# Token-mixing MLP beside attention: a scheduler that reckons weight loads 1.8 times as long, and its searched rules

## The chip, the cores and the metric

The kernel runs on one core of one Trainium2 chip. The metric is the device time of a launch in microseconds. A core has the engines PE (TensorE, matrix products), DVE (VectorE), ACT (ScalarE), POOL (GpSimd) and SP (SyncE, which here issues all transfers). Each has its own instruction queue, worked off in order; they meet only at semaphores.

## The reference

A layer norm without parameters feeds two branches, which are multiplied and added to the input. All tensors are bfloat16; S = 2048 tokens, D = 640, H = 32 heads of 20, F = 1536.

```python
def _A_ref(x, wqkv, wo):                       # attention
    qkv = (x @ wqkv).reshape(B, S, 3, H, Dh).transpose(2, 0, 3, 1, 4)
    q, k, v = qkv[0], qkv[1], qkv[2]
    scores = einsum("bhqd,bhkd->bhqk", q, k) * (Dh ** -0.5)
    p = softmax(scores, axis=-1)
    o = einsum("bhqk,bhkd->bhqd", p, v)
    return o.transpose(0, 2, 1, 3).reshape(B, S, D) @ wo

def _B_ref(x, w1, b1, w2, b2):                 # MLP over the tokens
    h = layernorm(x)
    u = gelu_tanh(einsum("bsd,sf->bdf", h, w1) + b1)
    y = einsum("bdf,fs->bds", u, w2) + b2
    return y.transpose(0, 2, 1)

xn = layernorm(A_x)
out = A_x + _A_ref(xn, A_wqkv, A_wo) * silu(_B_ref(xn, B_w1, B_b1, B_w2, B_b2))
```

The exponentials are the bulk: 32 heads x 2048 x 2048 scores.

## The kernel before

The kernel does not list its instructions in a fixed order. A Python program (the scheduler) runs when the kernel is built: it keeps an estimate of when each engine is free, chooses at each step the next piece of work for the engine that is free first, and so writes one fixed instruction order for each engine. What it decides by its estimates is frozen in these orders; on the chip only the semaphores act.

Scores are computed in units of one head x 128 keys x 512 queries, one bank of the accumulator memory each. There are 2048 such units. Most go to ACT, which takes the exponential of two or three banks in one instruction. 496 of them go to DVE instead, in quads of four heads: DVE converts a bank to a 16-bit number that, read as bfloat16, approximates the exponential (`emit_op1`), and derives from the four banks three shifted copies in one instruction each (`emit_top`); the four approximations are added with weights in the product with v.

```python
    def emit_exp():
        us, banks, grp = pexp.pop(0)
        n = len(us)                                        # 2 or 3 banks
        ...
        tk = pr.act(lambda e: e.activation(outp, inp, AF.Exp, scale=math.log(2.0) / 128.0), ...
                    cost=n * 512 * 0.8335 + 50.0)
    def emit_op1():
        tk = pr.dve(lambda e: e.tensor_scalar(w, src, WOFF, 0.0, ALU.add, ALU.max), ... cost=601.0)
    def emit_top():
        tk = pr.dve(lambda e: e.tensor_scalar(dst, src, dk, None, ALU.add), ... cost=dv(2048, .26))
```

The MLP's products fill PE in between. Its weights come in slices of 256 columns, w1 in six slices and w2 in eight, into two buffers used in turn: the load of slice k waits until the products of slice k - 2 have been read (`wr` holds the buffer's slot).

```python
        def dma_w1(k):
            src = B_w1[:, k * 256:(k + 1) * 256].rearrange("(b p) f -> p b f", p=P)
            dst = w1_ap(k)
            wr = [S_(f"wm{k % 2}")]
            return ("dma", lambda e: e.dma_start(dst, src), [], wr, f"dma_w1_{k}", S * 512,
                    [S_(f"x{b}") for b in range(NB)] if k < 2 else [])
        def dma_w2(k):
            ...
            return ("dma", lambda e: e.dma_start(dst, src), [], wr, f"dma_w2_{k}", F * 512,
                    [S_("wm0"), S_("wm1")] if k < 2 else [])
        ...
            if j % 2 == 1 and j // 2 + 2 < NB // 2:
                k = j // 2 + 2
                add_job(f"w2_{k}", [dma_w2(k), ("tag", f"w2_{k}")], (f"m2_{j}_0", f"m2_{j}_1"), 40.0)
```

The number in the sixth place (S * 512, F * 512) is the load's size in bytes as the scheduler reckons it; the true size is the same (2048 x 256 x 2 bytes for w1, 1536 x 256 x 2 for w2). It becomes a cost, and the cost a landing time. Times are in ns; `pipe` is the one pipe that all transfers share in the reckoning:

```python
        def dma(fn, reads, writes, name, nbytes, over=()):
            if nbytes is None:                             # the transposing DMAs
                pr.dma(fn, ..., cost=1320.0, over=over, tail=3200.0)
            else:
                pr.dma(fn, ..., cost=nbytes / 355.0, over=over)
    # in Prog._add, for a transfer:
            start = max(start, 700.0)
            if tail is not None:
                self.T[eng] = start + cost
                self.pipe = max(self.pipe, start) + cost
                t.fin = self.pipe - cost + tail
            else:
                self.T[eng] = start + 450.0
                self.pipe = max(self.pipe, start + 600.0) + cost
                t.fin = self.pipe + (1200.0 if self.pipe < 2500.0 else 2800.0 if cost > 800.0 else 1400.0)
```

All transfers are issued by SP in the order in which the scheduler made them. Among them are sixteen transposing DMAs, made in one piece when the attention output of the first six head groups is complete:

```python
        def reload_steps():
            steps = []
            for c in range(4):
                for tb in range(NTB):
                    ...
                    steps.append(("dma", lambda e, d=d, src=src: e.dma_start_transpose(d, src), ...))
```

The scheduler's rules of choice have fourteen parameters. A table gives their values for each window of 16 units of scores; each digit chooses one of the values of the option in that place:

```python
    OPTS = (
        ("SLACK", (120.0, 40.0, 200.0, 320.0)),
        ("MINJ", (640.0, 320.0, 1000.0)),
        ("ROOM", (3, 6, 0)),
        ...
        ("GROT", (1, 0)),
    )
    PLAN = (
        "00000000000010", "00000000000000", "00000000000010", ...      # 129 rows
    )
    def tune(self, w):
        if w < len(self.PLAN):
            for (name, vals), i in zip(self.OPTS, self.PLAN[w]):
                setattr(self, name, vals[int(i)])
    # in the main loop of schedule():
            if nclaim[0] >= win * self.WIN:
                self.tune(win)
                win += 1
```

The table was found by a search over the scheduler's own estimate. SLACK, for instance, is how far other PE work may overrun the moment at which ACT will need its next scores.

Of the kernel before, what the change touches and what calls it, by code (L numbers as in the profile page):

```python
# [260 lines left out]
class _Kern:  # L261
# [53 lines left out]
        ("GROT", (1, 0)),  # L315
    )
    PLAN = (
        "00000000000010", "00000000000000", "00000000000010", "00000000000000", "00000410000000", "10010410000100",
        "00004010011000", "20204010111000", "00000000000000", "02000020010010", "00000000000000", "00000010001000",
        "00000000000000", "01000120000000", "01003120000000", "00000000000000", "00000010000100", "00000310100000",  # L320
        "02020320011000", "02020320011000", "02120010011000", "00000220000100", "30000220000100", "02000010000000",
        "00000000000000", "00000000100000", "02000100100100", "01000120001010", "00000000000000", "00003300000000",
        "00000000000000", "01000000000010", "00004000000000", "10011000000000", "01022300000000", "00000000000000",
        "30020100000000", "02000010110000", "00000100000000", "00010100000110", "00001000000000", "20100000000100",
        "11000000000000", "00000000000000", "00001000010000", "10020000000000", "10020000010000", "10020010010000",
        "00000000000000", "22103000000000", "22103010000000", "01220100000100", "00000000000000", "00100000001000",
        "02000000100000", "01000300001000", "01000300001000", "00000000000000", "00100000001000", "00100400100000",
        "01000000001000", "00004000000000", "10002000010000", "01001400001010", "01021420000110", "00000300000000",
        "00000020000010", "00000000000000", "00000010001000", "10000100000000", "10000100000000", "10004100001000",
        "00004120000000", "00001010000000", "10011410000110", "11001200000110", "11001200100110", "00020000000000",  # L330
        "00000000000000", "00000000100100", "00200400100000", "02100010110010", "02101010100010", "01000000000000",
        "01000000000000", "00000000000000", "00000400000000", "00000000000000", "00000020001000", "00020320000000",
        "00000000000000", "01000010000000", "01000010000100", "20000000000100", "02000000000000", "12000000000000",
        "00001000101000", "00000000000000", "00200000010100", "00020020100000", "01003000000000", "22000000000000",
        "21210000000000", "00000000000000", "00200020110000", "00000000000000", "00200000000100", "00000000001000",
        "00020310000100", "00220020000010", "10224000000010", "31223410000010", "30200000000100", "00021000000010",
        "00100000001010", "01100000010010", "01204001000000", "01204100001000", "00204100000010", "02024120000000",
        "02024320000000", "02000200000000", "12000200010000", "00000000000000", "00001000100000", "00001000100000",
        "00000000001000", "10000000000000", "00000000000000",
    )  # L340
    PARTS = (2,)
    DX = (1, 2, 3)
# [74 lines left out]
    def schedule(self):  # L417
        pr, t, nc = self.prog, self.t, self.nc
        S, NB, NTB, F, FC, D, H, DH, NG, GH = (self.S, self.NB, self.NTB, self.F, self.FC, self.D,
                                               self.H, self.DH, self.NG, self.GH)  # L420
# [18 lines left out]
        def S_(name):  # L439
            s = sl.get(name)  # L440
            if s is None:
                s = sl[name] = _Slot(name)
            return s
# [321 lines left out]
        def w1_ap(k):  # L765
            return bass.AP(regA, (k % 2) * NB * 256, [[NB * 640, P], [256, NB], [1, 256]])

        def w2_ap(k):
            return bass.AP(regA, (k % 2) * FC * 256, [[NB * 640, P], [256, FC], [1, 256]])

        def dma_w1(k):
            src = B_w1[:, k * 256:(k + 1) * 256].rearrange("(b p) f -> p b f", p=P)
            dst = w1_ap(k)
            wr = [S_(f"wm{k % 2}")]
            return ("dma", lambda e: e.dma_start(dst, src), [], wr, f"dma_w1_{k}", S * 512,
                    [S_(f"x{b}") for b in range(NB)] if k < 2 else [])

        def dma_w2(k):
            src = B_w2[:, k * 256:(k + 1) * 256].rearrange("(fc p) s -> p fc s", p=P)
            dst = w2_ap(k)  # L780
            wr = [S_(f"wn{k % 2}")]
            return ("dma", lambda e: e.dma_start(dst, src), [], wr, f"dma_w2_{k}", F * 512,
                    [S_("wm0"), S_("wm1")] if k < 2 else [])

        def ztmp(i):
# [652 lines left out]
        for i, (b0, nb) in enumerate(LN):  # L1438
            rq = () if i < 4 else (f"xn{LN[i - 1][0] + LN[i - 1][1] - 1}",)
            steps = ln_steps(b0, nb)  # L1440
            k = next(n for n, x in enumerate(steps) if x == ("tag", f"lnp{b0}")) + 1
# [16 lines left out]
        for w in (1, 0):  # L1458
            src = A_wqkv[:, 640 * w + 256:640 * w + 640].rearrange("(kc p) f -> p kc f", p=P)
# [52 lines left out]
        for G in range(1, NG):  # L1512
            cs = sorted({(80 * G - 80) // 128, (80 * G - 1) // 128})
            for w in (1, 0):
# [4 lines left out]
            add_job(f"vs{G}", vs_steps(G, list(range(NR))), vtag + ((f"pvG{G - 2}",) if G >= 2 else ()), 28.0,  # L1519
                    at=(4 * G - 1.0 if G < NG - 1 else 24.0))  # L1520
        add_job("w1a", [dma_w1(0), dma_w1(1), ("tag", "w1_0"), ("tag", "w1_1")], ("h_all",) + xtall, 40.0)
        ml = []
        for j in range(FC):
            rq = ("h_all", "bias", f"w1_{j // 2}")
            ml.append((f"m1_{j}_0", mlp_steps(1, j, 0), rq, 16 * 216.0))
            if j % 2:
                ml.append((f"m1_{j}_1", mlp_steps(1, j, 1), rq + (f"m1_{j - 1}_0",), 32 * 60.0))
            if j % 2:
                add_job(f"a1_{j}", act_steps(1, j), tuple(f"m1_{i}_{q}" for i in (j - 1, j) for q in (0, 1)), self.ACTP)
            if j % 2 == 1 and j // 2 + 2 < FC // 2:  # L1530
                k = j // 2 + 2
                add_job(f"w1_{k}", [dma_w1(k), ("tag", f"w1_{k}")], (f"m1_{j}_0", f"m1_{j}_1"), 40.0)
        m1all = tuple(f"a1_{j}" for j in range(FC))
        m1pe = tuple(f"m1_{j}_{q}" for j in range(FC) for q in (0, 1))
        add_job("w2a", [dma_w2(0), dma_w2(1), ("tag", "w2_0"), ("tag", "w2_1")], m1pe, 40.0)
        for j in range(NB):
            rq = m1all + (f"w2_{j // 2}",)
            ml.append((f"m2_{j}_0", mlp_steps(2, j, 0), rq, 12 * 216.0))
            if j % 2:
                ml.append((f"m2_{j}_1", mlp_steps(2, j, 1), rq + (f"m2_{j - 1}_0",), 24 * 60.0))  # L1540
            if j % 2:
                add_job(f"a2_{j}", act_steps(2, j), tuple(f"m2_{i}_{q}" for i in (j - 1, j) for q in (0, 1)), self.ACTP)
# [3 lines that stand above are left out]
# [11 lines left out]
        for gb in range(4):  # L1557
            src = A_x[0, gb * 512:(gb + 1) * 512, :].rearrange("(b p) d -> p b d", p=P)
            dst = regA[:, gb * 4:(gb + 1) * 4, :]
# [377 lines left out]
        while True:  # L1937
# [40 lines left out]
            r, e = bt  # L1978
# [46 lines left out]
```

The softmax here doesn't subtract the row's maximum and nothing guards it: scores larger than these inputs give would overflow.

## Time and profile before

| | before |
|---|---|
| time, median of 3 runs | 757.67 us (757.1 to 758.49) |
| span of the profiled run | 756.4 us |
| exps on ACT, two banks / three banks | 434 / 228 |
| conversions on DVE, first / derived | 496 / 372 |
| transfers | 42.54 MB, mean 56 GB/s |

The span is that of one profiled execution. A group of instructions is shown as line, engine, operation, what it writes and reads, shape and count; then the busy time, the mean duration of one in ns, and the idle time of the engine just before them with what ended it. Durations of neighbours can overlap. In a timeline a line holds instructions of one kind merged, with their start, length and count. SPq is the queue of SP.

### The profile page before, as it was taken

To read this page: it belongs to the slowest core of one execution; us is meant where nothing else is said; L and a number is where in the kernel's file an instruction comes from. 1 tells how busy PE (TensorE), PEld (TensorE's weight loads), DVE (VectorE), ACT (ScalarE), POOL (GpSimd) and SP (SyncE) were. 2 spreads that over 40 slices of the span, in tenths; PEclk is the share of its full clock that TensorE was granted. 3 is DMA by queue.
4 is the path that set the end of the run, shared out by engine and by line. 5 is a ranking of instruction groups with operands and counts; after the bars stand their busy time and mean duration, and the time that the engine had idled before them with its cause. 6 is when DMAs were issued, how large, how long until landed. Compare 5 with 4: busy or idle time off the path is not lost.

```text
span 756.4 us, 22917 instructions
## 1 busy us (share of the span) xinstructions
PE 726.6 (96%) x10194; PEld 245.9 (33%) x10194; DVE 718.4 (95%) x1319; ACT 731.3 (97%) x686; POOL 15.7 (2%) x22
## 2 busy tenths in 40 slices
PE   8899999999999999999999989999999899999997
PEld 6332233222332323323232233333333333322232
DVE  7799999999999999999999999999999898999996
ACT  4999999999999999999999999999999999999994
POOL 4200000000000000000000000000000000000001
PEclk9999999999999999999999999999999999999999
DMA  8694111101120302203010131331134510410002
GB/s 240 89 160 88 41 20 37 21 13 30 37 63 12 76 13 44 62 26 76 13 39 13 37 91 31 69 80 29 45 81 76 104 50 2 152 47 29 31 13 70
DMA packets 117143, 42.54 MB, mean 56 GB/s; under 512 B 75300, under 2 KB 115876, under 8 KB 116996
## 3 DMA queue, kind: packets, MB, share of 16 engines
q1 hardware_dynamic: 117044, 41.07, 24.2%
q8 instruction: 80, 1.31, 0.8%
q14 instruction: 19, 0.16, 0.1%
HBM read 26.37 MB, written 10.22 MB: 48 GB/s over the span
## 4 chain that ended last, share of the span: by engine, by line
ACT 67%; PE 23%; SPq 4%; DVE 3%; DMA 3%; POOL 1%; issue 0%; DVEq 0%; ACTq 0%
ACT pt_sb L1241 65%; PE ps_all L1212 7%; PE ps_all L1292 7%; PE ps_all L645 7%; SPq L906 3%; DMA xnT_sb<-regC 1%; PE ps_all L930 1%; DMA regA<-in_B_w_dram 1%; ACT zt_sb L836 1%; DMA wqk_sb<-in_A_wqkv_dram 1%; DVE dt_sb L1252 1%; PE ps_all L630 1%; POOL st_sb L567 0%; SPq L1425 0%; DVE regC L1615 0%
## 5 line engine op out<-in xcount | busy, mean ns | idle before, releaser
L1241 ACT ACTIVATE pt_sb<-ps_all 128x1024 bf16<-128x1024 f32 (+1 forms) x662 | 711.5, 1212 | 3.9 <-PE ps_all L1212 2.9
L1252 DVE TENSOR_SCALAR dt_sb<-ps_all 128x512 uint16<-128x512 f32 x496 | 330.8, 681 | 17.1 <-PE ps_all L1212 15.6
L1212 PE MATMUL ps_all<-qk_sb 32*128 32x512 bf16 x2048 | 286.6, 384 | 18.7 <-ACT pt_sb L1241 14.5
L1276 DVE TENSOR_SCALAR dt_sb<-dt_sb 128x2048 uint16<-128x2048 uint16 x372 | 245.9, 684 | 1.6
L1212 PEld LDWEIGHTS ps_all<-qk_sb 32*128 32x128 bf16 x2048 | 73.9, 91 | 276.4 <-ACT pt_sb L1241 193.0
L1292 PE MATMUL ps_all<-pt_sb,v_sb 128*21 128x512 bf16 x1552 | 123.6, 382 | 1.0 <-DVE v_sb L1045 1.0
L1292 PE MATMUL ps_all<-dt_sb,vs_sb 128*21 128x512 bf16 x1488 | 123.6, 381 | 0.3 <-DVE dt_sb L1276 0.2
L645 PE MATMUL ps_all<-regB,regA 128*32 128x128 bf16 (+1 forms) x1536 | 66.8, 301 | 1.5 <-DMA regA<-in_B_w_dram 1.2
L645 PE MATMUL ps_all<-regC,regA 128*32 128x512 bf16 (+1 forms) x1536 | 65.9, 301 | 0.0
L1292 PE MATMUL ps_all<-dt_sb,v_sb 128*21 128x512 bf16 x496 | 48.9, 385 | 0.6 <-DVE tr_sb L1408 0.3
L645 PE MATMUL ps_all<-xnT_sb,wqk_sb 128*32 128x512 bf16 x640 | 48.9, 382 | 0.3 <-DVE v_sb L1045 0.2
L1292 PEld LDWEIGHTS ps_all<-pt_sb,v_sb 128*21 128x21 bf16 x1552 | 29.1, 90 | 50.6 <-issue 38.5
L1292 PEld LDWEIGHTS ps_all<-dt_sb,vs_sb 128*21 128x21 bf16 x1488 | 31.6, 91 | 38.2 <-issue 18.8
L645 PEld LDWEIGHTS ps_all<-regB,regA 128*32 128x32 bf16 x1536 | 28.1, 96 | 28.5 <-issue 12.2
L645 PEld LDWEIGHTS ps_all<-regC,regA 128*32 128x32 bf16 x1536 | 28.5, 96 | 25.7 <-issue 11.7
L930 PE MATMUL ps_all<-wv_sb,xnT_sb 128*128 128x128 bf16 (+3 forms) x160 | 30.1, 302 | 0.1
L645 PE MATMUL ps_all<-wv_sb,xnT_sb 128*32 128x480 bf16 x320 | 23.6, 369 | 0.2 <-DVE v_sb L1045 0.2
L1408 DVE STREAM_TRANSPOSE tr_sb<-ps_all 128x512 f32<-128x512 f32 x31 | 21.9, 707 | 0.0
L645 PEld LDWEIGHTS ps_all<-xnT_sb,wqk_sb 128*32 128x32 bf16 x640 | 14.3, 95 | 20.0 <-issue 8.7
L1292 PEld LDWEIGHTS ps_all<-dt_sb,v_sb 128*21 128x21 bf16 x496 | 12.4, 90 | 23.7 <-issue 18.3
L815 DVE TENSOR_SCALAR zt_sb<-ps_all,b2h_sb 128x512 bf16<-128x512 f32 (+1 forms) x32 | 17.2, 543 | 1.4 <-PE ps_all L645 1.2
L1045 DVE CAST v_sb<-ps_all 128x480 bf16<-128x480 f32 (+1 forms) x24 | 14.3, 594 | 2.3 <-PE ps_all L738 2.1
(81 smaller groups left out, 291.0 us busy)
## 6 DMA issues: line engine op xcount, KB each, us to landing
regA<-in_B_w_dram SPq DMA_DIRECT2D x6, 1024.0 KB
regA<-in_B_w_dram SPq DMA_DIRECT2D x8, 768.0 KB
qk_sb<-qk_scratch_dram SPq DMA_DIRECT2D x56, 80.0 KB
qk_scratch_dram<-qs_sb SPq DMA_DIRECT2D x32, 128.0 KB
regA<-in_A_x_dram SPq DMA_DIRECT2D x6, 640.0 KB
ok_scratch_dram<-on_sb SPq DMA_DIRECT2D x96, 20.0 KB
out_dram<-regC SPq DMA_DIRECT2D x3, 640.0 KB
wqk_sb<-in_A_wqkv_dram SPq DMA_DIRECT2D x2, 480.0 KB
```

The source lines that it names most:

```text
L630: steps.append(("pe", lambda e, dc=dc, lhsT=lhsT: e.matmul(ps(bk, n), lhsT, xnT_sb[:, dc, tb * 512 + c0:tb * 512 + c0 + n], start=(dc == 0 ...
L645: fns.append(lambda e, c=c, e_=e_: e.matmul(oc(c, e_), lhsT[:, c:e_], rhs, start=start, stop=stop, tile_position=(0, c)))
L815: steps.append(("dve", lambda e, z=z, i=i, jj=jj: e.tensor_scalar(z[:, c0:c0 + n], ps(bk, n, i * n), 0.5, bias[:, jj:jj + 1], ALU.mult, AL ...
L906: steps.append(("dma", lambda e, d=d, src=src: e.dma_start_transpose(d, src), [S_(f"okd{pass_of[(G, tb)]}_{g}") for G in range(L6) for g i ...
L930: steps.append(("pe", lambda e, c=c, k=k: e.matmul(ap, oT_sb[0:k, c, b * 128:(b + 1) * 128], wo_ap[0:k, c, c0:c0 + n], start=(opens and c ...
L1045: return lambda e: e.tensor_copy(dst, src)
L1212: pr.pe(lambda e, outp=outp, lhsT=lhsT, rhs=rhs, g=g: e.matmul(outp, lhsT, rhs, start=True, stop=True, tile_position=(32 * g, 0)), reads=[ ...
L1241: tk = pr.act(lambda e: e.activation(outp, inp, AF.Exp, scale=math.log(2.0) / 128.0), reads=[bank_slot[b] for b in banks[:n]], writes=[S_( ...
L1252: tk = pr.dve(lambda e: e.tensor_scalar(w, src, WOFF, 0.0, ALU.add, ALU.max), reads=[bank_slot[bk]], writes=[S_(f"dt{d['tl'][0]}_{g}")], n ...
L1276: tk = pr.dve(lambda e: e.tensor_scalar(dst, src, dk, None, ALU.add), reads=[S_(f"dt{b0}_{g}") for g in range(4)], writes=[S_(f"dt{b}_{g}" ...
L1292: pr.pe(lambda e: e.matmul(outp, lhsT, rhs, start=(k == 0), stop=last, tile_position=(0, 32 * g)), reads=reads, writes=[bank_slot[AB]], na ...
L1408: steps.append(("dve", lambda e: e.transpose(tr_sb[:, :], ps(AB)), [bank_slot[AB]], [S_("tr")], f"epT{q}", 632.0))
```

## The change

Two things. The loads of the MLP's weight slices are reckoned with 922 bytes per row in place of 512, which is 1.8 times the cost; their real size is unchanged. It is meant to bring the reckoned landing closer to what such loads take on the chip, so that the scheduler does not place a product before its weights are there. And the table of rules was searched anew with these costs.

```diff
     PLAN = (
-        "00000000000010", "00000000000000", "00000000000010", "00000000000000", "00000410000000", "10010410000100",
-        "00004010011000", "20204010111000", "00000000000000", "02000020010010", "00000000000000", "00000010001000",
 ... (all 129 rows; 7 are the same as before)
+        "00010000000000", "00000000000000", "00000000000010", "00000000000000", "01020420000000", "01210300000000",
+        "01110300000000", "01213210100000", "01000020000000", "01020020000110", "00200000110000", "02200200110000",
 ...
     )
@@ dma_w1
-            return ("dma", lambda e: e.dma_start(dst, src), [], wr, f"dma_w1_{k}", S * 512,
+            return ("dma", lambda e: e.dma_start(dst, src), [], wr, f"dma_w1_{k}", S * 922,
@@ dma_w2
-            return ("dma", lambda e: e.dma_start(dst, src), [], wr, f"dma_w2_{k}", F * 512,
+            return ("dma", lambda e: e.dma_start(dst, src), [], wr, f"dma_w2_{k}", F * 922,
```

No arithmetic changes. The instructions on PE, DVE, POOL and SP are the same in kind and number; their order differs, and with it the numbers of two-bank and three-bank exps on ACT.

More of the change, by code (lines that the diff above doesn't have):

```diff
@@ L317 @@
     PLAN = (
-        "00000000000010", "00000000000000", "00000000000010", "00000000000000", "00000410000000", "10010410000100",
-        "00004010011000", "20204010111000", "00000000000000", "02000020010010", "00000000000000", "00000010001000",
-        "00000000000000", "01000120000000", "01003120000000", "00000000000000", "00000010000100", "00000310100000",
-        "02020320011000", "02020320011000", "02120010011000", "00000220000100", "30000220000100", "02000010000000",
-        "00000000000000", "00000000100000", "02000100100100", "01000120001010", "00000000000000", "00003300000000",
@@ L323 @@
[L323 to L337, printed above, removed]
@@ L338 @@
-        "02024320000000", "02000200000000", "12000200010000", "00000000000000", "00001000100000", "00001000100000",
-        "00000000001000", "10000000000000", "00000000000000",
+        "00010000000000", "00000000000000", "00000000000010", "00000000000000", "01020420000000", "01210300000000",
+        "01110300000000", "01213210100000", "01000020000000", "01020020000110", "00200000110000", "02200200110000",
+        "02120020000000", "00000000000000", "00004020011000", "00004120011000", "00000000000000", "01104000000000",
@@ new lines @@
+        "10000100000010", "10000100000010", "10000110000110", "00000000000000", "02020000010000", "00012400100010",
+        "00000000000000", "00000300000000", "00000210000000", "20103210010000", "00100000000010", "20200000000000",
+        "00200300100000", "00003000000010", "00003100000010", "00003400000010", "01102400101010", "00000000000000",
+        "00002020010000", "30002010010000", "30102310010000", "10102310010000", "00000100000000", "01010110000010",
+        "10020000000000", "01003010000100", "00104000000100", "00120000000000", "00121010000000", "00000000000000",
@@ new lines @@
+        "00000010000000", "12000010000000", "10000020000000", "10202010000010", "10222010100010", "00000000000000",
+        "00002220000000", "00000000000000", "00003000010000", "00003200010100", "02000010000100", "20020000000000",
+        "00000000000000", "10100000000000", "10100010010100", "00001300000010", "00004200000010", "00201300001100",
+        "00201300000100", "00000000000000", "00000200000100", "00020200000110", "00010400100000", "10210100101000",
+        "10200100011000", "01020000000000", "00000220000000", "01000200010010", "22000010010010", "22000310010110",
@@ new lines @@
+        "02202000000000", "02212000100000", "00203000001000", "00000200001000", "00000000000000", "00001010001000",
+        "00002310101000", "00000110101000", "00000300000000", "01010300000000", "10000020000100", "00000000000000",
+        "00010000100000", "00001100000100", "01003100000100", "00000000000000", "00000410011000", "12000400110000",
+        "32000400110000", "00002000100000", "00002000100000", "20020000000000", "02100000000000", "00000020001010",
+        "00104020000000", "00000100000000", "02000110000000", "02003110001000", "02002120001000", "02002110001000",
@@ L340 @@
+        "22102100001000", "22203100001000", "22123100011100", "20200000100000", "20004200110000", "00000000000000",
+        "00004000000000", "00003000101100", "10003000101110", "10003000101110", "00000000000000", "00100020001000",
+        "20110010001100", "22220010001000", "22220010011000", "00000100000010", "00020000000000", "00220200110100",
+        "01220210110100", "11220210100100", "00000000000000",
     )
```

## The prediction

> **What bounds the kernel now.** I read the page's busy shares and its forty slices first, to see whether one engine rules. All three compute engines are nearly full for nearly the whole span, and the TensorE clock is granted in full, so the question is which of the three has least room.
>
> ```profile
> span 756.4 us, 22917 instructions
> PE 726.6 (96%) x10194; PEld 245.9 (33%) x10194; DVE 718.4 (95%) x1319; ACT 731.3 (97%) x686; POOL 15.7 (2%) x22
> PE   8899999999999999999999989999999899999997
> DVE  7799999999999999999999999999999898999996
> ACT  4999999999999999999999999999999999999994
> ```
>
> ScalarE (ACT) has its idle time only at the two ends. To get that in microseconds I cut the span in three: the start until the exps run without a break, the steady part, and the tail after the last exp.
>
> ```profile
> 0.00:38.50 38.50, 33.44 (x305) 19.54 (x306) 29.95 (x107) 26.83 (x28) 12.76 (x19) 1.00 0.76 167
> 38.50:746.00 707.50, 686.90 (x9863) 224.21 (x9860) 681.44 (x1197) 704.46 (x659) 0.63 (x1) 1.00 0.22 50
> 746.00:756.50 10.50, 6.30 (x31) 2.10 (x29) 6.99 (x16) 0.00 (x0) 2.26 (x2) 0.99 0.19 64
> ```
>
> The columns are length, then busy time of PE, its weight loads, DVE, ACT and POOL, clock, DMA share and GB/s. In the steady 707.5 us ACT is idle for 707.5 - 704.46 = 3.04 us, PE for 20.6 and DVE for 26.1. The chain of waits agrees: the exps of line 1241 hold 65% of it. So a change of order can gain only what ACT loses, and the groups by shape say what ACT has to do there:
>
> ```profile
> L1241 ACT ACTIVATE pt_sb<-ps_all 128x1024 bf16<-128x1024 f32 x424 | 424.6, 1066 | 0.8 <-PE ps_all L1212 0.4
> L1241 ACT ACTIVATE pt_sb<-ps_all 128x1536 bf16<-128x1536 f32 x219 | 327.0, 1493 | 1.9 <-PE ps_all L1212 1.3 <-PE ps_all L1292 0.3
> L841 ACT ACTIVATE zt_sb<-zt_sb 128x1280 bf16<-128x1280 bf16 x8 | 10.5, 1316 | 0.0
> L836 ACT ACTIVATE zt_sb<-zt_sb 128x1280 bf16<-128x1280 bf16 x6 | 7.8, 1304 | 0.0
> ```
>
> These durations overlap. From start to start, with nothing late between, the trace has 904 ns (median) for a two-bank exp, 1330 for a three-bank one, 1160 for a tanh. Least work in the steady part: 424 x 0.904 + 219 x 1.330 + 14 x 1.160, and 0.8 for two evictions, is 383.3 + 291.3 + 16.2 + 0.8 = 691.6 us. So ACT loses 707.5 - 691.6 = 15.9 us: 3.0 openly idle, 12.9 spread over exps that start a little late without a visible gap. That sum is the whole prize for a perfect schedule.
>
> The one open wait that the changed weight times bear on is found in the timelines of SyncE's queue, PE and ACT near 600 us:
>
> ```profile
> 571.78 22.60 SPq L906 DMA_TRANSPOSE xnT_sb<-ok_scratch_dram  x16
> 594.47 0.53 SPq L782 DMA_DIRECT2D regA<-in_B_w_dram  x1
> ```
> ```profile
> 601.09 0.83 PE L645 MATMUL ps_all<-regB,regA 128*32 128x512 bf16 x12 [1.21 <-DMA regA<-in_B_w_dram]
> ```
> ```profile
> 603.37 3.71 ACT L1241 ACTIVATE pt_sb<-ps_all 128x1536 bf16<-128x1536 f32 x3 [1.29 <-PE ps_all L1212]
> ```
>
> A w2 load is issued at 594.47, right behind sixteen transposing DMAs; the chain of waits gives it 6.57 us to land; PE stands 1.21 us for it, and ACT then has a gap of 1.29 us. That gap is 1.29 of the 3.04 us. No other weight load is waited for anywhere in the trace.
>
> [...] the load was delayed by what stood before it on SyncE, not by its own bytes.
>
> **The change part by part.**
>
> 1. The reckoned time of a load. The scheduler lets a large load land 600 + cost + 2800 ns after its issue. For w2 the cost was 1536 x 512 / 355 = 2215 ns, in all 5.6 us; now 1536 x 922 / 355 = 3989, in all 7.4. The one measured landing, 6.57, lies between: the old figure was 0.95 us short, the new one 0.8 us long. For w1 6.35 becomes 8.7 us. No instruction changes by this; it shifts where the scheduler puts the consumers.
>
> 2. The table of rules. Only 7 of its 129 rows are as before, so the whole order after the start is new. I compared the two programs' instruction orders, which carry no times. PE, DVE, POOL and SyncE have exactly the same instructions in the same numbers (2048 score matmuls, 496 first-key conversions on DVE and 372 derived ones, 100 filler matmuls, 298 DMAs). Only ACT differs: 425 two-bank and 234 three-bank exps in place of 434 and 228. That is 9 x 904 - 6 x 1330 = 156 ns less: -0.16 us. ACT's order is the same for its first 38 instructions, PE's for 165, DVE's for 129, so the start stays; the last 13 on PE, 20 on DVE and 11 on SyncE are also the same.
>
> 3. The weight stall. I count places in PE's order by score matmuls: about 2000 of them in 707.5 us, 0.354 us each. Before, the seventh w2 load may go once 1554 score matmuls are past, but the sixteen transposes become due at 1551 and stand ahead of it; the data is wanted at 1644, and the load lands at about that moment. After, the seventh load is due at 1533 and stands ahead of the transposes (due at 1555); it is the eighth that goes behind them, and that is first wanted at 1680. This is 36 places, 12.7 us, further on, while the transposes end at most 4 places, 1.4 us, later: some 11 us to spare. All other weight loads have at least 57 places (20 us) between release and use, against 6.57. So the wait should vanish: -1.3 us of ACT gap, -1.5 us with the late start hidden in the exp before it.
>
> 4. The tail. After the last exp the 10.5 us are a chain PE, DVE, store. The new order has two output-projection matmuls fewer between the last normalised block and the last products, but DVE runs through from 749.33 to 754.0 without a gap there, so I book 0. The order gives 12 last matmuls on exps instead of 4 behind a block of 7 others; this is even within some 0.3 us.
>
> 5. The other losses. Of ACT's 15.9 us, some 14.4 are not that stall. The new order has its own late exps, and their number doesn't follow from anything in the profile of before. PE's order has 1651 runs of equal instructions for 1640: a few more changes of shape, some 11 x 0.1 us of PE time (in the timeline four value matmuls are followed by four more after 0.23 us, by score matmuls after 0.32), against 20 us of PE idle time. I book 0 +/- 1.5 us.
>
> Sum: 757.67 - 1.5 - 0.16 + 0 = **756.0 us**; I say 756.2, since a fresh order may as well bring one stall that the old one, chosen from many, did not have.
>
> **The rivals.** (a) The search found a tighter order as well: ACT's 12.9 us of hidden lateness shrink by a fourth, -3 us more, 753. For it: the reckoned times are now nearer the measured ones, and the rules leave their defaults more often. Against it: the engine loads are equal to the instruction, so both searches came to the same split. (b) The longer reckoned loads cost freedom, or the new order holds stalls that the scheduler does not see: a score matmul or a DVE conversion late by 0.3 us in twenty places eats the gain and more, 759 to 761. For it: a stall of 0.62 us at 211 us and one of 0.69 at 740 in the order of before show that such things occur at random. Against: the weights have slack everywhere, so nothing forces it. (c) The wait only moves: the transposes now delay something else on SyncE, for example the reload of o. Its first reader, the output projection, stands at 1757, some 200 places (70 us) after the transposes, so I give this little.
>
> **Range and chances.** The certain parts are small (-1.7 us); the spread is that of step 5, about 2 us, and 0.7 us from run to run (757.1 to 758.49). So 753.6 to 758.8 for 8 in 10. Two per cent is 15 us, as much as all of ACT's loss: faster by that is next to impossible, 0.01; slower by it would need a lost engine, 0.01; within 2% 0.98.
>
> **What would show it.** Right: no wait of PE for a w2 load, the idle before the exps down from 3.9 us to about 2.5, the sixteen transposes still near 572 to 595 us, and the last exp ending near 744.5 us. The groups' counts 425 and 234 are given. Wrong: a new open gap on ACT of over 1 us; a steady part in which ACT's start-to-start losses differ from 15.9 - 1.5 us by more than 2; a tail longer or shorter than 10.5 us by over 0.5. If the weight stall is gone and the time is not lower, step 5 has failed.

## The result and the profile after

| | before | after |
|---|---|---|
| time, median of 4 runs each | 757.82 us (757.1 to 758.49) | 760.96 us (760.59 to 762.24) |
| ratio, 95% interval | | 1.0045 [1.0027, 1.0062] |
| span of the profiled run | 756.4 us | 759.2 us |
| last exp ends | 745.77 us | 749.01 us |
| ACT idle in front of its exps | 3.9 us | 6.8 us |

The change costs about 3 us. The page of the changed kernel looks like that of before: three full engines, and ACT with idle time at the two ends.

```profile
span 759.2 us, 22924 instructions
PE 730.3 (96%) x10194; PEld 247.2 (33%) x10194; DVE 720.7 (95%) x1319; ACT 732.2 (96%) x683; POOL 15.7 (2%) x22
ACT  5899999999999999999999999999999999999994
```

The difference is in two rows of the groups by line. For the exps the idle time before them is now 6.8 us, of which 5.6 for scores (L1212). For L930, the output projection, the idle time was 0.1 us before; now it is 1.3, and it waits for a transfer. Before:

```profile
L1241 ACT ACTIVATE pt_sb<-ps_all 128x1024 bf16<-128x1024 f32 (+1 forms) x662 | 711.5, 1212 | 3.9 <-PE ps_all L1212 2.9
L930 PE MATMUL ps_all<-wv_sb,xnT_sb 128*128 128x128 bf16 (+3 forms) x160 | 30.1, 302 | 0.1
```

After:

```profile
L1241 ACT ACTIVATE pt_sb<-ps_all 128x1024 bf16<-128x1024 f32 (+1 forms) x659 | 712.3, 1227 | 6.8 <-PE ps_all L1212 5.6
L930 PE MATMUL ps_all<-wv_sb,xnT_sb 128*128 128x128 bf16 (+3 forms) x160 | 31.3, 310 | 1.3 <-DMA xnT_sb<-oT_scratch_dram 1.3
```

No PE wait for a weight load is left: the old stall is gone, and another, for a different transfer, has come. I added up by how much every ACT start behind an exp or a tanh comes later than the least start-to-start time (904, 1330 and 1160 ns by shape), from the first exp to the last. This is ACT's loss: 17.15 us before, 21.04 after. With the 0.16 us that the counts of exps save, and a first exp 0.50 us earlier (13.60 us, 14.10 before), 3.89 - 0.16 - 0.50 = 3.23 us is the shift of the last exp. The tail after it gives 0.47 us back (10.66 to 10.19). By stretches of 40 us the loss falls by 1.85 us at 600 to 640 us, where the weight stall was, and rises by 2.2 at 640 to 680, by 1.4 at 280 to 320 and by 1.0 in the first 40; all other stretches change by 0.7 or less.

**The new stall.** SyncE's queue in the kernel before, around 642 us, has a block's store of attention output (L1432, 128 KB), its reload for the output projection (L892), and then four loads of the next layer part's x (L1560, 640 KB each):

```profile
642.21 0.36 SPq L1432 DMA_DIRECT2D oT_scratch_dram<-stage_sb  x1
644.07 0.68 SPq L892 DMA_DIRECT2D xnT_sb<-oT_scratch_dram  x1
644.80 2.41 SPq L1560 DMA_DIRECT2D regA<-in_A_x_dram  x4
```

The same queue in the changed kernel:

```profile
635.91 2.46 SPq L1560 DMA_DIRECT2D regA<-in_A_x_dram  x4
641.29 0.34 SPq L1432 DMA_DIRECT2D oT_scratch_dram<-stage_sb  x1
646.18 0.67 SPq L892 DMA_DIRECT2D xnT_sb<-oT_scratch_dram  x1
```

The x loads go into the buffer of the MLP's weights, and the new order finishes the MLP earlier (its last product stands at score matmul 1734 of 2048, before at 1760). So the loads leave first, and the small store follows behind 2.6 MB. Before, the reload could be issued 1.86 us after the store; now the chain of waits has

```profile
641.29 4.87 DMA oT_scratch_dram<-stage_sb
646.16 0.02 issue
646.18 3.04 DMA xnT_sb<-oT_scratch_dram
649.22 0.04 issue
649.26 0.39 PE ps_all L930
```

In front of the loads the store took 1.86 us to its reload's issue, behind them 4.87 us to land. For most of that time the DMA was at work on what had been queued before: it moved 359 GB/s from 641.2 to 645.2 us and 50 in the microsecond after. PE's and ACT's timelines at that place:

```profile
649.26 0.39 PE L930 MATMUL ps_all<-wv_sb,xnT_sb 128*128 128x512 bf16 x1 [1.29 <-DMA xnT_sb<-oT_scratch_dram]
649.59 0.39 PE L1212 MATMUL ps_all<-qk_sb 32*128 32x512 bf16 x3
653.64 0.61 PE L1212 MATMUL ps_all<-qk_sb 32*128 32x512 bf16 x3
```
```profile
650.02 3.28 ACT L1241 ACTIVATE pt_sb<-ps_all 128x1536 bf16<-128x1536 f32 x3 [0.67 <-PE ps_all L1212]
654.29 9.81 ACT L1241 ACTIVATE pt_sb<-ps_all 128x1024 bf16<-128x1024 f32 x9 [0.98 <-PE ps_all L1212]
```

PE stands 1.29 us, and ACT has a gap of 0.67. But four us later there is a second, larger gap without any wait for a transfer. The same three score matmuls take 0.61 us there instead of 0.39. The windows (columns as in the prediction: after POOL stand clock, DMA share and GB/s) say why: in the second one the mean granted clock is 0.58 and PE has no idle time at all. The clock record has 0.50 from 651.93 to 655.34 us and 1.00 on both sides, so 0.58 is a mean of the two.

```profile
648.00:652.00 4.00, 2.34 (x21) 0.97 (x22) 2.69 (x6) 3.33 (x4) 0.00 (x0) 0.99 0.04 15
652.00:656.00 4.00, 4.00 (x27) 0.93 (x25) 3.55 (x7) 2.96 (x4) 0.00 (x0) 0.58 0.00 2
```

In the 3.41 us before the fall PE worked 2.27 us. Idle time of that length alone doesn't account for it: in the kernel before PE worked only 1.54 of the 3.41 us up to 601.09, the end of its wait for the weights, and the clock stayed at 1.00. What makes it fall is not shown.

### The profile page after: what moved, and what is told of

Read it like the earlier page. It is cut to its first block, busy times and chain, and to the rows that moved or that the text cites. A ratio compares the mean times of both kernels' runs of the same rounds, so it can differ in the third digit from the quotient of the medians.

```text
span 759.2 us, 22924 instructions
## 1 busy us (share of the span) xinstructions
PE 730.3 (96%) x10194; PEld 247.2 (33%) x10194; DVE 720.7 (95%) x1319; ACT 732.2 (96%) x683; POOL 15.7 (2%) x22
## 4 chain that ended last, share of the span: by engine, by line
ACT 74%; PE 20%; DVE 3%; DMA 2%; POOL 0%; issue 0%
ACT pt_sb L1241 72%; PE ps_all L1212 6%; PE ps_all L1292 5%; PE ps_all L645 5%; PE ps_all L930 1%; PE ps_all L1317 1%; ACT zt_sb L841 1%; PE ps_all L630 1%; DVE dt_sb L1252 1%; DMA xnT_sb<-regC 1%; DMA oT_scratch_dram<-stage_sb 1%; ACT zt_sb L836 1%; DVE dt_sb L1276 1%; DMA xnT_sb<-oT_scratch_dram 0%; POOL st_sb L567 0%; DVE regC L1615 0%
## 5 line engine op out<-in xcount | busy, mean ns | idle before, releaser
L1212 PE MATMUL ps_all<-qk_sb 32*128 32x512 bf16 x2048 | 290.0, 385 | 18.6 <-ACT pt_sb L1241 14.0
L1212 PEld LDWEIGHTS ps_all<-qk_sb 32*128 32x128 bf16 x2048 | 74.6, 91 | 279.1 <-ACT pt_sb L1241 187.1
L1292 PE MATMUL ps_all<-dt_sb,vs_sb 128*21 128x512 bf16 x1488 | 125.8, 382 | 0.2 <-DVE dt_sb L1276 0.2
L645 PE MATMUL ps_all<-regB,regA 128*32 128x128 bf16 (+1 forms) x1536 | 68.8, 300 | 0.0
L930 PE MATMUL ps_all<-wv_sb,xnT_sb 128*128 128x128 bf16 (+3 forms) x160 | 31.3, 310 | 1.3 <-DMA xnT_sb<-oT_scratch_dram 1.3
L645 PE MATMUL ps_all<-wv_sb,xnT_sb 128*32 128x480 bf16 x320 | 21.5, 369 | 0.0
```

What stands on the lines that cost most here:

```text
L645: fns.append(lambda e, c=c, e_=e_: e.matmul(oc(c, e_), lhsT[:, c:e_], rhs, start=start, stop=stop, tile_position=(0, c)))
L930: steps.append(("pe", lambda e, c=c, k=k: e.matmul(ap, oT_sb[0:k, c, b * 128:(b + 1) * 128], wo_ap[0:k, c, c0:c0 + n], start=(opens and c ...
L1212: pr.pe(lambda e, outp=outp, lhsT=lhsT, rhs=rhs, g=g: e.matmul(outp, lhsT, rhs, start=True, stop=True, tile_position=(32 * g, 0)), reads=[ ...
L1292: pr.pe(lambda e: e.matmul(outp, lhsT, rhs, start=(k == 0), stop=last, tile_position=(0, 32 * g)), reads=reads, writes=[bank_slot[AB]], na ...
```

## The experiments

Theory A: the loads of x, released earlier, hold up the store; that wait and the slow clock behind it cost more than the weight stall did. Rivals: B, the longer reckoned times themselves do harm; C, the new table is a worse order in many places; D, most of the loss is the clock, which filler matmuls would keep up. The ratios are against runs of the kernel before beside each group: medians 757.12, 756.58 and 757.24 us in the three groups, in the order in which they are told.

**table_alone: the new table, the old reckoned times**

```diff
-   f"dma_w1_{k}", S * 922,        # and F * 922 for w2
+   f"dma_w1_{k}", S * 512,        # and F * 512
```

> The new table of rules with the old reckoned load times. The scheduler writes the very same four instruction orders as with the new load times, so it is the changed kernel under another text. Theory A (the whole change lies in the table, the reckoned times do nothing once the table is fixed): 760.5 to 762, like the changed kernel. Rival B (something else in the text matters): a time nearer 758. It also serves as a second profile of the changed order: if the slow TensorE clock at 20 to 24 us and at 652 to 656 us, and the half-microsecond hole inside four equal matmuls at 288.9 us, belong to the order, they come again; if they were chance, they do not.

759.9 us (757.67 to 762.1), ratio 1.0030 [1.0019, 1.0041]. This comes out as the same program as the change, instruction for instruction: with this table the reckoned times change neither the order nor the scheduler's estimate of the end. The run is therefore a second sample of the change. Its chain has the stall again, somewhat larger. PE waited about 2.3 us, from the end of its last score matmuls at 646.33 to the landing of the reload at 648.63:

```profile
639.65 6.02 DMA oT_scratch_dram<-stage_sb
645.68 2.95 DMA xnT_sb<-oT_scratch_dram
```

ACT's loss at 640 to 680 us is 3.84 us here, 2.76 in the first profile and 0.56 before. Rival B falls for this table. The window at 20 to 24 us has its full clock here (1.00; in the first profile 0.57), with the same order, so the 1.0 us lost in the first 40 us was chance of that one run.

**cost_alone: the old table, the new reckoned times**

```diff
-   f"dma_w1_{k}", S * 512,        # and F * 512 for w2
+   f"dma_w1_{k}", S * 922,        # and F * 922
```

> The new reckoned load times with the old table of rules. The scheduler's own estimate of the end goes from 743.5 to 746.9 us (for the changed kernel it is 744.6). Theory A (the old table is fitted to the old reckoned times; with others its rules fall in the wrong places): slower than before by about the 3.3 us of the estimate, 760 to 762. Rival B (truer load times are worth having by themselves, the 1.5 us stall behind the transposes goes and nothing else is lost): 756 to 757.

758.35 us (757.94 to 761.08), ratio 1.0019 [1.0009, 1.0028]: +1.2 us by the medians, where the scheduler's own estimate rises by some 3.3 (743.5 to 746.9). Both forecasts missed. Under this table the times do change the order: the profile has no wait of PE for a weight load any more, but its tail after the last exp is 11.49 us, 10.66 before. That the old table was fitted to the old times agrees with the estimate; no run takes the 1.2 us apart.

**w2_ahead: the kernel before, with the late weight load put ahead of the sixteen transposes**

```diff
+   w = next(t for t in sp if t.name == "dma_w2_6")
+   # its own semaphore d8; the products that read it wait for d8 too
+   sp.remove(w); sp.insert([t.name for t in sp].index("oTt0_0"), w)
```

> The kernel before, and one thing changed in SyncE's order: the seventh w2 load is issued before the sixteen transposing DMAs, not after them. All other orders stay. This is the stall that the longer reckoned times were meant against, taken away alone. Theory A (that stall costs 1.3 us of ACT gap and 0.2 hidden): 756.0 to 756.6, no wait of PE for a w2 load, no ACT gap near 603 us. Rival B (the gap is absorbed later, because PE or DVE are behind ACT anyway): 757.3 or more.

756.51 us (755.85 to 758.07), ratio 0.9993 [0.9983, 1.0003]. This does by hand the one good thing that the change did. SyncE's queue shows the load in its new place:

```profile
571.53 0.49 SPq L782 DMA_DIRECT2D regA<-in_B_w_dram  x1
572.06 25.43 SPq L906 DMA_TRANSPOSE xnT_sb<-ok_scratch_dram  x16
```
```profile
599.55 13.05 ACT L1241 ACTIVATE pt_sb<-ps_all 128x1536 bf16<-128x1536 f32 x12
```

and ACT runs on where it had its gap of 1.29 us. Its loss falls by 1.38 us between 600 and 640 us. In all it falls by 0.91 (17.15 to 16.24), but the rest is lost in the first 40 us (1.69 to 2.17), ahead of anything that the edit moves. The time falls by 0.6 us, less than the 1.5 that my step 3 booked, with an interval that runs from 1.3 us to no gain.

**x2_behind: the changed kernel, with the four x loads put behind the store and the reload**

```diff
+   i = [t.name for t in sp].index("x2_0")
+   x, b = sp[i:i + 4], sp[i + 4:i + 6]     # four x loads; the store, the reload
+   # the store takes over the waits of x as well
+   sp[i:i + 6] = b + x
```

> The changed kernel, and one thing changed in SyncE's order: the four 640 KB loads of x for the last addition are issued after, not before, the store and reload of the attention output of one block. All other orders stay. Theory A (the four loads hold up the small store, 4.9 us instead of 1.9, PE waits 1.3 us for it and then runs at half clock for 3 us): the wait and the slow clock near 650 us go, 2 us less, 758.7 to 759.3. Rival B (the wait only uncovers another one right behind, or ACT catches up): 760.5 or more.

757.57 us (756.96 to 759.48), ratio 1.0006 [0.9994, 1.0019], 2.3 us under table_alone on the same chip and lower than theory A had forecast.

```profile
639.43 0.35 SPq L1432 DMA_DIRECT2D oT_scratch_dram<-stage_sb  x1
641.31 0.67 SPq L892 DMA_DIRECT2D xnT_sb<-oT_scratch_dram  x1
642.07 2.67 SPq L1560 DMA_DIRECT2D regA<-in_A_x_dram  x4
```
```profile
652.00:656.00 4.00, 3.71 (x34) 1.20 (x31) 4.00 (x9) 4.00 (x5) 0.00 (x0) 1.00 0.02 4
```

The store is home after 1.88 us, PE doesn't wait for the reload, the clock stays at 1.00 and ACT is busy all 4.00 us of the window. ACT's loss in 640 to 680 us is 0.67, against 2.76 and 3.84 in the two profiles of the changed order so far. This shows theory A, and its size: 2.3 of the change's 2.8 us in this group.

**stall_fill: the changed kernel, with 24 filler matmuls in front of the waiting product**

```diff
+   i = ...   # the PE task that waits for the reload oTl70_4_48
+   pe[i:i] = [_Task("pe", "pe", fn[k % 4].fn, "pvz") for k in range(24)]
```

> The changed kernel with 24 filler matmuls (zero weights, added to the open accumulator of the value product) put on PE just before the output-projection matmul that waits for the reloaded block; the collision with the loads of x stays. Theory A (part of the loss at 650 us is not the wait but the half clock that follows it): the wait shrinks by the fillers' time of about 1.3 us and lands at the same moment, the clock at 652 to 656 us stays full, and the time is 0.8 to 1.2 us under that of the changed order (759.9 in the last series), 758.7 to 759.1. Rival B (the clock falls for another reason, or the wait itself is all of it): within 0.4 us of 759.9.

758.59 us (757.77 to 762.4), ratio 1.0024 [1.0011, 1.0037]. The clock was 1.00 from 648 to 656 us, as meant, but fell to 0.68 at 640 to 644, ahead of the fillers, so this one didn't tell what the clock alone is worth. It is 2.0 us above the kernel before of its group; table_alone was 2.8 above that of its own.

**x2_two_ahead: two of the x loads ahead of the store, two behind**

```diff
-   sp[i:i + 6] = b + x
+   sp[i:i + 6] = x[:2] + b + x[2:]
```

> The changed kernel with two of the four 640 KB loads of x ahead of the store, and two behind its reload. Theory A (what holds the store up is the bytes still queued in front of it: four loads take 7 to 8 us and two take 4, and the store comes 5.4 us after the first load): the store lands in about 2 us as without loads, PE does not wait, 757.3 to 758.2, like the order with all four behind. Rival B (any large load in front, or the order of the semaphores, costs the wait): 759 or more.

757.04 us (756.67 to 757.83), ratio 1.0009 [1.0001, 1.0016].

```profile
634.30 1.27 SPq L1560 DMA_DIRECT2D regA<-in_A_x_dram  x2
639.69 0.34 SPq L1432 DMA_DIRECT2D oT_scratch_dram<-stage_sb  x1
641.55 0.67 SPq L892 DMA_DIRECT2D xnT_sb<-oT_scratch_dram  x1
```

The two loads leave 5.4 us before the store, as the four did in the changed kernel (635.91 and 641.29), but the store is home in 1.86 us. It is the bytes still queued that hold it, not the place behind a load as such: in the 5.4 us from the first load's issue to the store's the changed kernel's DMA moved some 1.3 MB (245 GB/s as a mean), which is two loads and half of the four.

**w2_ahead_fill: w2_ahead, with twelve fillers in the start**

```diff
+   patch_w2(pr); patch_fill(pr, "xTd5", 3)   # fillers before the first wait for xT
```

> The kernel before with the seventh w2 load ahead of the transposes, and 12 filler matmuls on PE in the start, where it waits for the transposed block of x near 19 us. In some profiles TensorE falls to half clock after that wait, in others not, with the same order. Theory A (the slow start comes from that wait, and is a matter of chance by some 0.5 us in the transfers): the runs above 758 us vanish, median 755.8 to 756.4. Rival B (the fillers delay the work behind them when the data is early): 756.6 or more.

756.55 us (756.21 to 758.04), ratio 1.0003 [0.9995, 1.0011]. Fillers at the start gain nothing that could be measured: the slow clock at 20 us stands in only one profile, the first of the changed kernel (0.57 from 20 to 24 us, where ten others have 1.00). The moved load is in this kernel too, and its 0.6 us doesn't show here; w2_ahead itself was not timed in this group, so what the fillers cost is not known.

**no_table: the kernel before, with an empty table**

```diff
-   PLAN = ("00000000000010", ... 129 rows)
+   PLAN = ()
```

> The kernel before with an empty table: the rules keep their defaults throughout. The scheduler's own estimate of the end is 762.6 us against 743.5 with the table, 19 us more. Theory A (the estimate orders tables rightly, to within the transfers it misjudges by a microsecond or two): 774 to 780 us. Rival B (a good part of what a search gains is fitted to the estimate and is not there on the chip): 763 to 772.

775.03 us (773.69 to 775.91), ratio 1.0242 [1.0228, 1.0256]: +18.4 us by the medians, where the estimate rises by 19.1. The estimate is thus good for large differences between orders. For the two tables, each with the times it was searched with, it gives 743.5 (before) and 744.6 us (after), some 1.0 more. The new table comes to 744.6 with either set of times, so by the old times the new order was the slower one. The search reckoned with the new times; by them the old table comes to 746.9, and the new one looked 2.3 us better.

**change_again: the changed kernel once more, and two repeats beside it.** No edit.

> The changed kernel itself, timed beside the two below in one series. Theory (the stall at the reload and the clock that falls after it explain 2.3 of its loss): 2.5 to 3.3 us over the kernel before, and a low granted clock in most of its runs.

760.14 us (757.22 to 762.04), ratio 1.0035 [1.0023, 1.0046]: 2.9 us over the kernel before, as forecast. The chain again has the store and the reload, and the clock again falls behind them:

```profile
639.97 6.10 DMA oT_scratch_dram<-stage_sb
646.08 2.79 DMA xnT_sb<-oT_scratch_dram
```
```profile
652.00:656.00 4.00, 4.00 (x30) 1.00 (x28) 3.42 (x6) 2.92 (x4) 0.00 (x0) 0.65 0.00 0
```

**w2_again: w2_ahead repeated.** Same edit.

> The kernel before with the seventh w2 load ahead of the transposes, once more, since the first series left 0.6 us less with an interval that reaches no change. Theory A (the stall is worth something): 0.4 to 1.2 us under the kernel before. Rival B (it is absorbed): within 0.3 us of it.

756.35 us (755.82 to 757.36), ratio 0.9985 [0.9977, 0.9993]: faster than the kernel before, by 0.9 us. In this profile ACT's loss is 15.80 us in all, 1.35 less than before, and 1.39 less at 600 to 640 us, so nothing of the gain is given back later. The lowest median of the study is that of the old order with one load moved.

**fill_again: stall_fill repeated.** Same edit.

> The changed kernel with 24 fillers ahead of the waiting matmul, once more, now beside the changed kernel itself. Theory A (the half clock after the wait is part of the loss): 0.6 to 1.4 us under the changed kernel of this series, and fewer runs with a low clock. Rival B: within 0.3 us of it.

759.55 us (758.05 to 761.42), ratio 1.0028 [1.0016, 1.0040], 0.6 us under change_again.

```profile
646.17 1.48 PE L1307 MATMUL ps_all<-wp_sb,zw_sb 128*21 128x512 bf16 x24
```
```profile
652.00:656.00 4.00, 3.48 (x35) 1.19 (x33) 4.00 (x9) 4.00 (x4) 0.00 (x0) 1.00 0.02 4
```

The fillers take up the wait (0.4 us is left of it), the clock is 1.00 and ACT is full in that window; ACT's loss at 640 to 680 us is 1.68: under the 2.76, 3.84 and 3.73 of the three profiles of the changed order (the first, table_alone, change_again), and over the 0.67 of x2_behind. The clock has a share in the 2.3 us, by these profiles half to two thirds of what ACT loses there. But this profile is of one of the two fastest of ten runs, and the times (0.6 us here, with overlapping intervals) don't settle the share. Rival D as the whole cause is unlikely: taking the wait away brought 2.3 us, filling it some 0.6.

## Why the prediction was wrong

756.2 us was predicted, with a range up to 758.8; it became 760.96. By its own steps:

1. **The reckoned time: no effect of its own.** table_alone is the same program, so the new times act through the search alone. That w1's and w2's reckoned landing was moved to the far side of the measured 6.57 us neither helped nor hurt this order.

2. **The table: right.** The counts 425 and 234 are there, and the start is the same up to chance (full clock in table_alone, 0.57 for 4 us in the first profile).

3. **The weight stall: right in kind, its size perhaps too large.** The wait is gone and with it ACT's gap. The term was booked at 1.5 us. Moving the load alone brought 0.6 and 0.9 us in two series (w2_ahead, w2_again), while their profiles show 1.38 and 1.39 us gained on the spot. The profile of before, against which these are taken, is a single run, and whether its stall is larger than usual is not shown.

4. **The tail: booked 0 within 0.3, measured -0.47 us.** Off by little, in the good direction.

5. **The other losses: this step failed.** Booked 0 +/- 1.5 us, on the ground that they don't follow from anything in the profile of before. A large part did. The order of SyncE's instructions was at hand, and it has the four x loads change places with a store and a reload which the output projection waits for. The collision behind that costs 2.3 us (x2_behind against table_alone), more than the step's whole allowance and more than the gain of step 3. Rival (c), "the wait only moves", was looked for behind the transposes only, where there was slack of 70 us, and given little; I didn't ask what an earlier end of the MLP would set free. Rival (b), new stalls unseen by the scheduler, 759 to 761 us, is what happened, though mainly as one large stall and not as twenty small ones.

Why did the scheduler not see it? It let the store land 4.2 us after its issue and the reload 2.2 after that; measured were 4.87 and 3.04, in all 1.5 us more. In its estimate PE waits some 0.3 us there; on the chip it was 1.29 us and more. That is the same kind of error as the one the change repaired for weights, in the transfers it left alone.

The sum: of 2.8 us (table_alone over before, medians) the collision makes 2.3. Without it x2_behind stands 1.06 us above w2_ahead, which is the old order without the weight stall. The scheduler's estimates of the two tables differ by 1.0 as well. This agreement is argued, not shown: the excess lies at about 190, 288, 455 and 572 us; the gap on ACT near 288 us comes in all seven profiles of the new order (0.25 to 0.69 us), so it belongs to the order, but no run here took its cause apart. change_again also has a gap on ACT of 1.02 us at 713.06, behind a second fall of the clock (0.91 as a mean from 700 to 720 us). There is no such fall in the first profile or in fill_again (1.00 there), and the run means of the three others with the loads moved or the wait filled (0.999, 0.999, and 0.998 in stall_fill with its fall at 640 to 644) leave no room for another 3.41 us at half clock; table_alone's mean, 0.996 like change_again's, does. What brings it stays open, and it may be a part of the 2.3 us.

## What to carry to other kernels

When a buffer comes free earlier, ask which large loads that lets go, and which small store with a waiting reader then stands behind them: compare the DMA queue's order of the two programs, not only that of the engines. Mend the reckoned times of all transfers together, by measured landings under load (not tried here); with one corrected alone, this search went where the others were still wrong. Before running a newly searched table, put its estimate beside that of the old table with the same times for both, the old and the new: where the two comparisons disagree, as here, the gain may lie in the reckoning alone, and moving the one late load by hand was the cheaper and the better cure.

## What the hardware showed that I had not expected

- A 128 KB store took 1.86 us to its reload's issue when the DMA had been all but idle (5 GB/s from 639 to 642.2 us in the kernel before), and 4.87, 6.02 and 6.10 us to land behind four 640 KB loads whose issue had ended about 3 us before. From the issue of the first load to the landing of the store it is 10.3 us (635.91 to 646.16), for 2.62 MB of loads some 256 GB/s as a mean. Behind two loads, issued 5.4 us ahead, the same store took 1.86 us.
- In the profiles of before and after TensorE's clock is recorded at 1.00 or 0.50, and both falls of the changed kernel that end inside the span last 3.41 us. The one behind the wait came at 651.93 us; the means of the windows (0.86 and 0.71 in table_alone, 0.92 and 0.65 in change_again, from 648 to 652 and from 652 to 656 us) put it at about 650.9 and 651.4 in the other two profiles of the changed order. That is 2.2 to 2.7 us after waits of 1.3 to 2.3 us had ended, at a time when PE was no longer idle. With fillers in the wait the clock stayed at 1.00 from 648 to 656 us. The length of a wait alone doesn't decide it: no fall followed the 1.21 us at 601 us in the kernel before, and stall_fill had one ahead of the fillers (0.68 from 640 to 644 us) where fill_again, the same program, had 1.00.
- One program spreads more than the other: the changed order ran from 757.22 to 762.04 us in change_again, w2_again from 755.82 to 757.36. A fall of 3.41 us to 0.50 takes 0.0023 off the mean clock of a run of 757 us; the one that ran into the end of the changed kernel's first profile (0.50 from 757.74 to 759.2) took 0.0010. The mean was 0.997 or less in 24 of 37 timed runs of the changed order (table_alone, change_again), in 4 of 21 with the wait filled, in 3 of 26 with loads of x moved behind the store, and in 10 of 131 of the kernel before. In the three profiles of the changed order the wait of 1.3 to 2.3 us thus cost once for itself and again for the 3.41 us at half clock behind it.
